# One PSUM tile with five banks, against separate PSUM tiles and another fixed order

## The chip, the cores and the metric

The kernel runs on one core of a Trainium2 chip. The time is device microseconds of one execution. Before the change, three executions took 315.47, 315.55 and 319.2 us, a median of 315.55 us. One of them was recorded by the profiler; all durations below come from that one.

## What is computed

A retention layer with a recurrent state, then a layer norm without offset, a two-layer perceptron with ReLU, and a residual. Inputs are float32.

```
q, k, v: (4, 8, 768, 64)             # batch, heads, sequence, head dim
gamma = 1 - 2 ** (-5 - arange(8))    # one per head
for t in range(768):
    state = gamma * state + k[t] (outer) v[t]
    y[t] = q[t] @ state / 8
x = y as (4, 768, 512)
xn = (x - mean) / sqrt(var + 1e-6) * g_ln
out = x + relu(xn @ w_ch1) @ w_ch2   # 512 -> 2048 -> 512
```

## The kernel before

**Tiles.** A batch has 6 chunks of 128 positions, so there are 24 tiles. Tiles 0 to 3 are the first chunks of the four batches, 4 to 8 are chunks 1 to 5 of batch 0, 9 to 13 those of batch 1, and so on.

**The steps of one tile t.** Loads of q, k, v go out on POOL's queue (float32 to bfloat16 in the DMA, L422); later ones are paced by a one-element copy on POOL that waits for an earlier load (L435). Tiles 0 to 7 have q and k transposed on TensorE (L488, L495) and evacuated by VectorE with a scaling (eq, L500) and by ACT (ek, L250). From tile 8 on SP transposes them by DMA (tr, L510) and VectorE scales (eq, L517). Then:

- *pa*: the scores, eight matmuls with 64 rows, two heads at a time, into two banks (L528).
- *am*: VectorE multiplies the scores by a decay mask into `asb` (L553).
- *ps*: from tile 8 on, the state's part of y, eight matmuls with 64 rows and 64 columns that stand ahead of pa and write the two banks of y (L539). Tiles 4 to 7 have it as four full-row matmuls in py (L575).
- *py*: eight matmuls that add the scores times v (L564; L579 up to tile 7).
- *bn*: VectorE's statistics of y (L595, L596). *xn*: VectorE's normalisation without the 1/sqrt (L607). *xc*: ACT copies y into `x_all`, for the residual (L614). From tile 8 on, y lies in two banks, so that bn, xn and xc have two instructions each.
- *vg*, *pd*, *pb*: POOL scales v (L628), TensorE adds the chunk's k times v into the state's bank (L640), VectorE scales that into one of two `state` tiles for the next chunk (L654).
- *tx*, *ex*: up to tile 7 xn is transposed on TensorE (L667) and copied by ACT (L250); later SP transposes it by DMA into `xnt` (L681).

**The perceptron.** Tiles go in groups: eight of one tile, four of two, two of four. M1 multiplies w1 by a group's xnt, in units of four 512-column matmuls' worth, into one of two `mm` buffers (L714), and ACT, or VectorE for some early ones, writes the ReLU into `h1` (L727, L729). M2 multiplies a tile's h1 by w2, sixteen matmuls in four quarters of four (L752), into one bank. Then *add* (L762) applies the 1/sqrt of the group (L689, L695), adds `x_all` and writes `osb`, and SP stores it (L769). The last tile's M2 is cut in 384 and 128 columns.

**PSUM.** `pd` has one bank, `mm` two. The other five are slices of a single tile, `banks`, with the names b0, b1, b2, p0, p1:

```
BANKS = ("b0", "b1", "b2", "p0", "p1")
TWO = [("b0", "b1")]
banks = ctx.enter_context(tc.tile_pool(name="banks", bufs=1, space=ps)).tile(
    [P, len(BANKS), 4 * P], FP32, name="banks")
```

pa takes p0 and p1. py takes b2 up to tile 7 and b1 and b2 after. The transposes take b0 or b1. M2 takes b0 or b1 for tiles 0 to 3, b0 for tiles 4 to 15 and any of the five from tile 16 on; which one is a digit of the order.

**The order.** Every step is a task given to `Plan.add` with its engine, a duration, what it comes after and which buffers it uses. A list of numbers, `ORDER`, says in which order the tasks of all engines, loads included, are written down. `Plan.order` walks through it with a small model of times and buffers, and `Plan.fill` uses these times to put matmuls on zeros (`warm`, L780) into TensorE's idle time in the first 14 us. Each engine runs its tasks in that order. The waits between engines are put in by the tile framework, by the tiles that instructions read and write; the plan's own list of what a task comes after makes none.

Of the kernel before, what the change touches and what calls it, by code (L numbers as in the profile page):

```python
# [22 lines left out]
    "load_pad": 600, "w_pad": 550, "lead": 32, "lead2": 32, "sq_at": 28000, "late_load": 1250, "two": 4, "m2b": ("b0",), "m2all": 16, "inter": 4, "every": 4, "tail": (0, 384, 512), "step": 8, "pace": 8, "ahead": 3,  # L23
# [6 lines left out]
3 2 15 18 19 23 24 0 5 6 4 8 7 16 20 1 17 22 14 21 10 27 26 25 146 100147 29 30 9 148  # L30
149 11 150 162 153 44 100163 151 28 13 32 164 45 33 154 100176 165 155 152 156 179 177
166 100158 157 167 168 159 31 178 214 169 170 100190 180 191 193 12 100172 171 524 181
192 46 174 173 182 183 194 532 204 34 184 35 36 47 38 100186 215 207 187 10525 10533 39
37 534 217 185 40 42 49 41 234 50 542 48 205 195 51 206 196 535 526 543 540 52 197 527
251 53 198 10541 54 43 208 55 216 528 209 200 544 100224 199 529 10545 201 188 227 536
537 225 226 210 550 175 211 552 228 212 229 551 553 546 220 213 221 218 100241 10547 219
548 242 556 10549 230 275 560 243 244 231 232 235 557 558 236 56 245 561 559 554 59 57
233 555 237 246 58 268 60 530 100258 247 238 562 531 248 570 252 259 261 563 249 260 566
571 564 262 239 567 254 565 250 160 256 255 568 538 100716 263 10569 253 10539 717 718
722 264 61 719 723 62 161 189 265 63 64 298 65 66 266 287 720 269 724 725 578 100271 726  # L40
572 727 721 307 276 267 270 728 272 202 573 579 278 299 277 279 67 71 729 730 731 280
574 72 576 300 222 575 240 732 281 734 282 284 288 223 577 203 283 735 736 273 285 290
68 289 69 70 301 291 737 584 582 738 292 302 740 741 77 742 293 743 294 295 296 297 585
78 73 74 303 308 75 318 319 310 309 322 744 580 286 746 333 311 304 76 83 747 312 320 84
79 581 748 305 583 749 313 314 588 316 315 745 733 339 317 334 602 323 325 589 750 324
592 752 80 350 603 753 257 335 326 81 306 327 328 329 331 600 754 340 82 755 593 739 321
354 85 601 351 586 330 89 332 337 587 342 756 86 341 90 87 758 594 88 91 368 595 92 336
95 596 379 93 338 352 96 343 344 274 355 345 94 346 382 97 98 99 101 102 380 348 397 759
100 760 590 761 597 347 103 349 357 591 107 356 598 381 762 358 610 764 359 599 360 361
765 766 383 604 767 362 363 369 364 371 751 386 403 370 611 763 384 768 614 605 372 608  # L50
770 373 771 374 375 398 609 615 606 366 377 757 353 365 376 618 378 772 387 389 388 390
108 104 607 619 773 105 774 404 106 113 414 418 775 612 616 109 110 114 429 111 112 115
391 116 456 119 392 120 117 776 613 617 393 395 118 394 620 777 396 622 621 623 399 406
405 778 626 407 415 408 419 409 410 627 433 624 625 412 779 416 628 634 401 411 769 145
385 417 445 413 400 421 420 430 121 122 123 125 126 780 127 782 783 629 635 422 431 367
423 784 630 424 785 425 427 426 428 631 124 632 131 132 129 459 402 434 457 786 436 435
788 437 432 465 789 646 633 438 128 476 130 647 790 650 133 458 446 439 440 791 441 442
443 651 638 448 792 447 449 639 640 460 794 461 641 781 444 450 466 451 452 454 480 644
645 795 453 477 796 636 455 468 467 797 637 478 469 642 648 462 643 798 137 134 138 491
143 135 139 136 492 470 800 495 787 471 481 793 140 472 474 649 473 652 475 653 801 802  # L60
662 483 663 482 666 803 667 658 484 506 659 141 485 142 144 656 804 806 657 486 496 487
488 489 493 654 660 807 490 655 661 498 497 808 809 510 499 479 799 511 463 670 671 810
500 664 507 824 665 501 502 503 504 668 508 672 505 669 513 673 512 825 674 678 464 514
515 300818 675 826 679 676 400812 677 682 680 813 819 814 494 516 683 681 517 519 509
518 521 684 686 520 685 687 815 690 805 811 691 696 820 697 702 522 694 703 695 100830
704 705 827 831 698 699 688 689 821 706 707 200854 692 816 523 822 693 708 300848 832
828 710 833 709 700 701 836 711 400842 849 843 712 714 850 837 817 823 829 715 713 834
838 839 851 855 844 845 852 856 840 835 853 857 846 860 841 861 847 862 858 863 864 859
865
# [3 lines left out]
class Plan:  # L73
# [6 lines left out]
    def __init__(self, seen, begin, first_load):  # L80
        self.seen, self.begin, self.first_load = seen, begin, first_load
        self.tasks, self.bufs, self.chosen = [], {}, {}
# [4 lines left out]
    def add(self, eng, ns, rank, emit, after=(), takes=None, uses=(), load=0, hw=0, lat=0, at=0,  # L87
            follows=(), slack=0, slots=None):
        after = [d for x in after for d in (x if isinstance(x, list) else [x])]
        t = {"on": eng if isinstance(eng, dict) else {eng: ns}, "rank": rank, "emit": emit,  # L90
             "after": after, "takes": takes, "uses": list(uses) + ([takes] if takes else []),
             "slots": (slots or [(takes[0],)]) if takes else [],
             "load": load, "hw": hw, "lat": lat, "at": at, "follows": list(follows),
             "slack": slack}
        self.tasks.append(t)
        return t

    def order(self, seq):
# [7 lines left out]
        for number in seq:  # L106
# [7 lines left out]
            for options in t["slots"]:  # L114
# [20 lines left out]
            for name in got:  # L135
# [3 lines left out]
                self.chosen[t["takes"]] = name  # L139
# [21 lines left out]
def kernel(  # L161
# [33 lines left out]
    T0, TX, T_TWO = CFG["T0"], CFG["TX"], CFG["two"]  # L195
# [16 lines left out]
    BANKS = ("b0", "b1", "b2", "p0", "p1")  # L212
    TWO = [("b0", "b1")]

    def make_pool(name, n, space=None):
# [7 lines left out]
        for name, n, space in (  # L223
# [3 lines left out]
            ("pd", 1, ps), ("mm", 2, ps),  # L227
        )
    }
    for name in BANKS:  # L230
        plan.pool(name, 1)
    plan.pool("pb", 2)
    held = {}
    banks = ctx.enter_context(tc.tile_pool(name="banks", bufs=1, space=ps)).tile(
        [P, len(BANKS), 4 * P], FP32, name="banks")

    def bank(key, bf16=False):
        x = banks[:, BANKS.index(plan.chosen[key])]
        held[key] = x.bitcast(BF16)[:, 0:4 * P].rearrange("p (i t) -> p i t", t=P) if bf16 else x
        return held[key]  # L240
# [4 lines left out]

    def heads(x):
        return x.rearrange("p (i a d) -> p i a d", a=2, d=D)
# [28 lines left out]
    bns = const.tile([P, NT, 2, 6], FP32, name="bns")  # L276
    mv = const.tile([P, NT, 2], FP32, name="mv")
    touch = const.tile([P, KO, 1], FP32, name="touch")
# [172 lines left out]
    a(SP, 390, -140, lambda eng: nc.sync.dma_start(out=touch, in_=w1_v[:, :, 0:1]), hw=300)  # L451

    unit, u, behind = {}, 0, []
    for g in range(NG):
        for ho in range(HO):
            unit["1", g, ho] = u
            u += GROUPS[g] / 4
            every = CFG["every"] if GROUPS[g] == 1 else 8 if 12 <= G0[g] < 16 and GROUPS[g] == 2 else 4
            if g >= CFG["inter"] and ho % every == every - 1 and behind:
                unit["2", behind.pop(0)] = u  # L460
                u += 4
# [14 lines left out]
    for t in range(NT):  # L476
# [7 lines left out]
        if t < T0:  # L484
            def e_tk(eng, t=t):
                p = bank(("tp", ("k", t)), True)
                for i in range(NPAIR):
                    nc.tensor.transpose(p[:, i, :], tile_of("k", t)[:, 2 * i:2 * i + 2, :], idn)  # L488
            tk = a(PE, 230, r - 0.1, e_tk, [loaded["k", t], ident] + ([tq] if tq else []),
                   ("tp", ("k", t)), [where["k", t]], slots=TWO)  # L490

            def e_tq(eng, t=t):
                p = bank(("tp", ("q", t)), True)
                for i in range(NPAIR):
                    nc.tensor.transpose(p[:, i, :], tile_of("q", t)[:, 2 * i:2 * i + 2, :], idn)  # L495
            tq = a(PE, 230, r, e_tq, [loaded["q", t], ident, tk], ("tp", ("q", t)),
                   [where["q", t]], slots=TWO)
# [25 lines left out]
        def e_pa(eng, t=t):  # L523
            pa = held["pa", t] = banks[:, 3:5].rearrange("p a (i t) -> p a i t", t=P)
            for i in range(NPAIR):
# [6 lines left out]
        pat = a(PE, 410, r + 1.2, e_pa, [eq, ek], ("pa", t), [("trq", t), kt], slack=slack,  # L532
                slots=[("p0",), ("p1",)])

        def e_ps(eng, t=t):
            for i in range(NPAIR):
                for par in range(2):
                    o = slice(D * par, D * (par + 1))
                    nc.tensor.matmul(  # L539
                        banks[:, 1 + par, i * D:(i + 1) * D], lhsT=held["trq", t][o, i, :],  # L540
                        rhs=held["pb", t][o, i, o], start=(i == 0), stop=False)
        pst = None
        if t >= T0:
            pst = a(PE, 120, r + 1.1, e_ps, [eq] + ([pbt[t]] if c > 1 else []), ("py", t),
                    [("trq", t), ("pb", t)], slots=[("b1",), ("b2",)])
            pat["after"].append(pst)
# [13 lines left out]
        def e_py(eng, t=t, c=c):  # L560
            if t >= T0:
                held["py", t] = banks[:, 1:3, 0:NPAIR * D].rearrange("p a (i d) -> p i a d", d=D)
                for h in range(H):
                    nc.tensor.matmul(  # L564
                        banks[:, 1 + h % 2, h // 2 * D:(h // 2 + 1) * D],
# [34 lines left out]
        for a2 in (range(2) if late else [None]):  # L600
            def e_xn(eng, t=t, a2=a2):
                if not a2:
                    take("xn", t, [P, DM], BF16)
# [212 lines left out]
```

## Time and profile before

| | |
|---|---|
| time of the profiled execution | 315.47 us |
| its span, first to last instruction | 313.7 us |
| granted TensorE clock, mean | 0.951 |
| asb, L553, x24 | 1223 ns each |
| osb (add), L762, 512 columns, x23 | 749 ns each |
| xn, L607: 512 columns x8; 256 columns x32 | 751; 481 ns each |
| bns, L595: 512 columns x8; 256 columns x32 | 698; 422 ns each |
| mv, L596: one part x8; two parts x16 | 182; 209 ns each |
| x_all, L614: 512 columns x8; 256 columns x32 | 588; 374 ns each |
| M2, L752, 512 columns, x368 | 389 ns each, mean |
| load of a part of w to landing, x8, median | 8.4 us |
| tr; xnt by DMA to landing, median | 3.6; 2.4 us |

A row of a group gives the line in the kernel, the engine, the operation, what it writes and reads, how often, its busy time and the mean of one. PE is TensorE's matmuls, PEld its weight loads, DVE VectorE, ACT ScalarE, POOL GpSimd, SP the sync engine's queue. Matmuls are pipelined and their ends are modelled: a single 512-column matmul reads some 380 ns while the next one starts 216 ns later. Idle time of an engine is given with the last thing that it waited for, as "X <- Y", or in brackets in the timeline.

### The profile page before, as it was taken

Reading aid. Unit: us, or ns where it says so; the run is one execution under the profiler, and the core shown is the slowest. Engines: PE = TensorE matmul, PEld = TensorE weight load, DVE = VectorE, ACT = ScalarE, POOL = GpSimd, SP = SyncE. Lnnn points to the kernel's source line nnn. Section 1 sums busy time; section 2 is a strip of 40 time slices with the busy share of each in tenths; the row PEclk is TensorE's granted clock in tenths of the full one; section 3 lists DMA queues with packets and bytes.
Section 4 is the critical chain, followed back from the end, with each engine's and each line's share of the span. In section 5 each row is a group of like instructions: output and inputs, shape, how many; then the busy total and the mean of one; then the engine's idle time right before and its main releaser. Section 6 shows DMA issues by size and latency. Waiting matters only on the chain. (4 is left out here: it accounts for less than half of the span.)

```text
span 313.7 us, 4959 instructions
## 1 busy us (share of the span) xinstructions
PE 230.5 (73%) x2029; PEld 141.6 (45%) x2029; DVE 124.7 (40%) x265; ACT 81.9 (26%) x170; POOL 97.5 (31%) x151
## 2 busy tenths in 40 slices
PE   3964676788867576768678687676977887699973
PEld 1433575677444244525446464444633433244431
DVE  3423445562454325544426454647326342002013
ACT  3122233246003202203103333213322232243200
POOL 9985561257014056406423533423000000000000
PEclk9997579999999997978999999999999999799999
DMA  9999998099209159969929996884910000201013
GB/s 135 169 187 171 199 163 101 3 69 70 17 20 163 20 35 159 123 75 117 100 84 87 87 133 84 67 103 61 176 50 11 8 17 0 87 0 67 33 37 134
DMA packets 108890, 26.82 MB, mean 85 GB/s; under 512 B 101569, under 2 KB 105921, under 8 KB 108866
## 3 DMA queue, kind: packets, MB, share of 16 engines
q0 software_dynamic: 77024, 13.37, 54.5%
q1 hardware_dynamic: 30642, 12.79, 18.7%
q10 hardware_dynamic: 1200, 0.33, 0.5%
q8 instruction: 16, 0.26, 0.4%
q14 instruction: 8, 0.07, 0.1%
HBM read 27.27 MB, written 6.29 MB: 107 GB/s over the span
## 5 line engine op out<-in xcount | busy, mean ns | idle before, releaser
L752 PE MATMUL banks<-w,h 128*128 128x512 bf16 (+2 forms) x400 | 97.1, 380 | 32.0 <-DVE xn L607 9.2
L714 PE MATMUL mm<-xnt,w 128*128 128x128 bf16 (+2 forms) x896 | 101.8, 268 | 7.3 <-DMA xnt<-xn 4.7
L714 PEld LDWEIGHTS <-w 128*128 128x128 bf16 x896 | 70.4, 103 | 30.8 <-issue 10.3
L727 ACT ACTIVATE h<-mm 128x512 bf16<-128x512 f32 x88 | 51.3, 600 | 84.9 <-PE mm L714 84.9
L752 PEld LDWEIGHTS <-h 128*128 128x128 bf16 x400 | 38.0, 99 | 75.3 <-issue 41.9
L553 DVE TENSOR_TENSOR asb<-banks,mask 128x1024 bf16<-128x1024 f32 x24 | 29.4, 1223 | 53.1 <-PE banks L752 31.6
L628 POOL TENSOR_TENSOR vg<-vsb,vsc 128x512 bf16<-128x512 bf16 x16 | 16.6, 1038 | 95.2 <-PE pd L640 86.0
L762 DVE SCALAR_TENSOR_TENSOR osb<-banks,rstd,x_all 128x512 f32<-128x512 f32 (+2 forms) x25 | 18.2, 728 | 60.5 <-ACT h L727 25.8
L614 ACT CAST x_all<-banks 128x256 bf16<-128x256 f32 (+1 forms) x40 | 15.8, 417 | 96.5 <-PE banks L752 28.6
L595 DVE BATCH_NORM_STATS2 bns<-banks 128x6 f32<-128x256 f32 (+1 forms) x40 | 17.8, 477 | 38.9 <-PE banks L752 26.9
L607 DVE SCALAR_TENSOR_TENSOR xn<-banks,mv,gb 128x256 bf16<-128x256 f32 (+1 forms) x40 | 20.5, 535 | 17.2 <-ACT x_all L614 7.3
L422 POOL DMA_DIRECT2D vsb<-in_v_dram x20 | 18.1, 908 | 1.5 <-issue 1.4
L654 DVE TENSOR_TENSOR state<-pd,gch 64x256 bf16<-64x256 f32 x40 | 16.7, 417 | 1.9 <-PE pd L640 1.5
L422 POOL DMA_DIRECT2D qk<-in_q_dram x16 | 14.5, 908 | 1.0 <-issue 0.8
L422 POOL DMA_DIRECT2D qk<-in_k_dram x16 | 14.3, 893 | 0.9 <-issue 0.8
L250 ACT COPY trk<-banks 128x512 bf16<-128x512 bf16 x8 | 4.7, 587 | 24.7 <-PE banks L488 7.9
L539 PE MATMUL banks<-state,trq 64*128 64x64 bf16 x128 | 4.9, 194 | 7.9 <-ACT x_all L614 5.6
L564 PE MATMUL banks<-vsb,asb 128*128 128x64 bf16 x128 | 6.4, 193 | 5.0 <-DVE asb L553 3.5
L780 PE MATMUL pd<-zeros 128*128 128x512 bf16 (+1 forms) x27 | 8.8, 481 | 1.2 <-DVE zeros L285 1.2
L564 PEld LDWEIGHTS <-asb 128*128 128x128 bf16 x128 | 5.5, 98 | 9.1 <-DVE asb L553 6.6
L539 PEld LDWEIGHTS <-trq 64*128 64x128 bf16 x128 | 3.7, 95 | 12.6 <-issue 7.0
L528 PE MATMUL banks<-trq,tr 64*128 64x128 bf16 x128 | 6.6, 222 | 2.7 <-DVE osb L762 2.7
(68 smaller groups left out, 140.7 us busy)
## 6 DMA issues: line engine op xcount, KB each, us to landing
out_dram<-osb SPq DMA_DIRECT2D x23, 256.0 KB, 2.3
w<-in_moe_w_ch_dram POOLq DMA_DIRECT2D x8, 512.0 KB, 8.4
vsb<-in_v_dram POOLq DMA_DIRECT2D x20, 128.0 KB, 4.5
qk<-in_k_dram POOLq DMA_DIRECT2D x16, 128.0 KB, 3.8
qk<-in_q_dram POOLq DMA_DIRECT2D x16, 128.0 KB, 3.7
qsb<-in_q_dram POOLq DMA_DIRECT2D x7, 128.0 KB, 7.2
v<-in_v_dram POOLq DMA_DIRECT2D x4, 128.0 KB, 5.7
ksb<-in_k_dram POOLq DMA_DIRECT2D x4, 128.0 KB, 8.6
```

Of the source, the lines that this page charges most:

```text
L422: nc.gpsimd.dma_start(out=tile_of(kind, j), in_=src)
L553: nc.vector.tensor_tensor(out=take("asb", t, [P, NPAIR, 2, P], BF16).rearrange("p i a t -> p a i t"), in0=held["pa", t], in1=mask.rearrang ...
L564: nc.tensor.matmul(banks[:, 1 + h % 2, h // 2 * D:(h // 2 + 1) * D], lhsT=held["asb", t][:, h // 2, h % 2, :], rhs=tile_of("v", t)[:, h, : ...
L595: nc.vector.bn_stats(out=bns[:, t, i, :], in_=x)
L607: nc.vector.scalar_tensor_tensor(out=dst, in0=src, scalar=mv[:, t, 0:1], in1=g, op0=ALU.subtract, op1=ALU.mult)
L614: nc.scalar.copy(out=dst, in_=src)
L628: e.tensor_tensor(out=take("vg", j, [P, H, D], BF16), in0=tile_of("v", j), in1=vsc[:, cc, :].unsqueeze(2).to_broadcast([P, H, D]), op=ALU. ...
L654: nc.vector.tensor_tensor(out=held["pb", n][o, :, o], in0=held["pd", b][o, :, o], in1=gch[o, cc, :].unsqueeze(2).to_broadcast([D, NPAIR, D ...
L714: nc.tensor.matmul(p[:, j, :], lhsT=w1[:, ko, (ho + j) * P:(ho + j + 1) * P], rhs=held["xnt", hb][:, h0:h0 + n, ko, :], start=(ko == 0), s ...
L727: nc.scalar.activation(out=dst, in_=src, func=AF.Relu)
L752: nc.tensor.matmul(held[key][:, 0:w], lhsT=held["h1", hb][:, ho, i * P:(i + 1) * P], rhs=w2[:, ho, cols], start=(ho == 0), stop=(ho == HO ...
L762: nc.vector.scalar_tensor_tensor(out=take("osb", key, [P, w], FP32), in0=held[key][:, 0:w], scalar=rstd[:, t:t + 1], in1=x_all[:, t, cols] ...
```

## The change

- The tile `banks` goes. Three pools come in its place: `tp` with two banks (transposes and all of M2), `pa` with one buffer of two banks, `py` with one bank. With `pd` and `mm` that makes eight banks, as before. `Plan` loses the choice of a bank (`slots`, `chosen`), and the settings `two`, `m2b`, `m2all`, `inter` and `every` go.
- y lies in one bank for every tile. The task ps goes; from tile 4 on py has the four full-row state matmuls itself. bn, xn and xc are one task each with 512 columns.
- The ranks that M2 tasks get (`unit`) are worked out in another way; with a fixed `ORDER` they move nothing.
- `ORDER` is another list, and with it the order on every engine, of the loads and of the gates. POOL's first load is k of tile 1; w2's last part stands behind vg of tile 1. The number of warm matmuls follows from the plan.
- The load named `touch` takes 16 columns of w1 where it took 1, and stands elsewhere on SP's queue.

```diff
 ORDER = [int(x) for x in """
-3 2 15 18 19 23 24 0 5 6 4 8 7 16 20 1 17 22 14 21 10 27 26 25 146 100147 29 30 9 148
+15 18 14 23 3 8 19 2 27 24 13 26 22 25 44 16 17 45 0 4 7 6 5 28 146 20 21 9 147 10 149 1
...
-            ("pd", 1, ps), ("mm", 2, ps),
+            ("tp", 2, ps), ("pa", 1, ps), ("py", 1, ps), ("pd", 1, ps), ("mm", 2, ps),
...
-    banks = ctx.enter_context(tc.tile_pool(name="banks", bufs=1, space=ps)).tile(
-        [P, len(BANKS), 4 * P], FP32, name="banks")
...
-    a(SP, 390, -140, lambda eng: nc.sync.dma_start(out=touch, in_=w1_v[:, :, 0:1]), hw=300)
+    a(SP, 390, -140, lambda eng: nc.sync.dma_start(out=touch, in_=w1_v[:, :, 0:16]), hw=400)
...
-                p = bank(("tp", ("k", t)), True)
+                p = take("tp", ("k", t), [P, NPAIR, P], BF16)
...
-            pa = held["pa", t] = banks[:, 3:5].rearrange("p a (i t) -> p a i t", t=P)
+            pa = take("pa", t, [P, 2, NPAIR, P], FP32)
...
-        def e_ps(eng, t=t):
-            for i in range(NPAIR):
-                for par in range(2):
-                    o = slice(D * par, D * (par + 1))
-                    nc.tensor.matmul(
-                        banks[:, 1 + par, i * D:(i + 1) * D], lhsT=held["trq", t][o, i, :],
-                        rhs=held["pb", t][o, i, o], start=(i == 0), stop=False)
...
-            py = bank(("py", t)).rearrange("p (h d) -> p h d", d=D)
+            py = take("py", t, [P, H, D], FP32)
             n = H + (NPAIR if c > 0 else 0)
             mi = 0
             if c > 0:
                 for i in range(NPAIR):
                     nc.tensor.matmul(py[:, 2 * i:2 * i + 2, :], lhsT=held["trq", t][:, i, :],
                                      rhs=held["pb", t][:, i, :], start=(mi == 0), stop=False)
                     mi += 1
...
+        def e_xn(eng, t=t):
+            nc.vector.scalar_tensor_tensor(
+                out=take("xn", t, [P, DM], BF16), in0=held["py", t].rearrange("p h d -> p (h d)"),
+                scalar=mv[:, t, 0:1], in1=gb, op0=ALU.subtract, op1=ALU.mult)
+
         def e_bn(eng, t=t):
-            parts = [banks[:, 1 + a, 0:NPAIR * D] for a in range(2)] if t >= T0 else [
-                held["py", t].rearrange("p i a d -> p (i a d)")]
-            for i, x in enumerate(parts):
-                nc.vector.bn_stats(out=bns[:, t, i, :], in_=x)
-            nc.vector.bn_aggr(out=mv[:, t, :], in_=bns[:, t, 0:len(parts), :])
+            nc.vector.bn_stats(out=bns[:, t, :], in_=held["py", t].rearrange("p h d -> p (h d)"))
+            nc.vector.bn_aggr(out=mv[:, t, :], in_=bns[:, t, :])
...
+        def e_xc(eng, t=t):
+            nc.scalar.copy(out=x_all[:, t, :].rearrange("p (h d) -> p h d", d=D),
+                           in_=held["py", t])
...
             def e_m2(eng, hb=hb, i=h0 + i4, key=key, part=part, cols=cols, w=w):
                 if part == 0:
-                    bank(key)
+                    take(*key, [P, w], FP32)
```

## The prediction

> **What bounds the kernel now.** I read the page first, its busy table and its 40 slices (7.84 us each):
>
> ```profile
> PE 230.5 (73%) x2029; PEld 141.6 (45%) x2029; DVE 124.7 (40%) x265; ACT 81.9 (26%) x170; POOL 97.5 (31%) x151
> ...
> PEclk9997579999999997978999999999999999799999
> DMA  9999998099209159969929996884910000201013
> ```
>
> then the busy times of three stretches, cut where the first M2 matmul starts (79.23 us) and where the last group's M1 starts (269.32 us); after each engine's busy time come clock, DMA share, GB/s:
>
> ```profile
> core 0: us, PE busy (x) PEld busy (x) DVE busy (x) ACT busy (x) POOL busy (x), PEclk, DMA share, GB/s
> 0.00:79.23 79.23, 53.67 (x653) 42.65 (x654) 32.84 (x75) 27.36 (x55) 48.48 (x71) 0.89 1.33 126
> 79.23:269.32 190.09, 139.53 (x1204) 82.11 (x1202) 85.70 (x180) 44.99 (x98) 48.98 (x80) 0.97 0.63 75
> 269.32:313.70 44.38, 37.26 (x176) 16.88 (x176) 6.19 (x10) 9.52 (x17) 0.00 (x0) 0.96 0.16 57
> ```
>
> No engine is full, and after 47 us the DMA engines are not either. TensorE is nearest, and 50.5 of its 83 idle us lie in the middle stretch. So I asked for whom it waits there (engine, line, who was waited for: total us, times, longest):
>
> ```profile
> PE banks L752 <- DVE xn L607: 9.2, 7, 1.8
> PE banks L752 <- DVE asb L553: 8.5, 8, 1.4
> PE banks L752 <- ACT x_all L614: 5.6, 6, 2.0
> PE banks L539 <- ACT x_all L614: 5.6, 7, 1.4
> PE mm L714 <- DMA xnt<-xn: 4.7, 1, 4.7
> PE banks L564 <- DVE asb L553: 3.5, 4, 1.3
> PE banks L752 <- DVE osb L762: 2.8, 2, 2.2
> PE banks L528 <- DVE osb L762: 2.7, 3, 0.9
> PE pd L640 <- DVE state L654: 2.4, 1, 2.4
> PE banks L752 <- DVE bns L595: 1.7, 2, 0.9
> ```
>
> L752 is M2. It multiplies h1 by w2 into a bank of its own; nothing in it needs the scores (asb), the normalised rows (xn), the copy x_all or the statistics (bns) of another tile, which lie in other banks. All five banks are slices of one tile, `banks`, and the program waits per tile. The built instruction list confirms it: of 34 M2 waits on VectorE's counter, 24 stand at a later quarter of a tile, where the bank is already held. The clearest place is after the last y (L564, ended 256.88):
>
> ```profile
> 256.48 0.40 PE L564 MATMUL banks<-vsb,asb 128*128 128x64 bf16 x8
> ...
> 264.68 0.76 DVE L595 BATCH_NORM_STATS2 bns<-banks 128x6 f32<-128x256 f32 x2 [8.43 <-PE banks L752]
> ...
> 269.32 2.29 PE L714 MATMUL mm<-xnt,w 128*128 128x512 bf16 x5 [4.67 <-DMA xnt<-xn]
> ```
>
> VectorE could have read y at 256.9; it waited until unrelated M2 matmuls ended, 7.8 us later. M1, which needs what follows, then idled 4.67 us.
>
> **The change, part by part.**
>
> *Pools for the one tile.* Scores, y, and the transposes with M2 get tiles of their own. In the changed program's list M2 has 22 waits on VectorE, each at a tile's first quarter, on the add that frees its bank. Waits of asb, bns, xn on M2 go from 25 to 0, those of ACT's copies from 20 to 0. Gone in the middle: 9.2+8.5+5.6+1.7 = 25.0 at M2; 2.2 of the 2.8 on osb (one quarter mid-tile); 2.7 (L528 on osb, another bank) and a 1.5 (L564 on osb); the 4.7 on xnt, which followed from the late statistics. Sum 36.1 us. In the tail L752 waits for osb five times, 4.1 us, again at later quarters or another bank, and M1 ran its first eight matmuls in 3.4 us at half clock after the idle 4.67, against 1.73 for later eights: 1.7 us. What is next where a stall goes: TensorE's own next task, since the order lists M1 or M2 quarters there.
>
> *State part of y.* Before, eight 64-row matmuls (L539), 0.12 us from their start to the scores' start. After, four full-row ones ahead of y, as L575 in tiles 4 to 7: y with them takes 0.46 us to the next task, without 0.23. So +0.11 us on TensorE for each of 16 tiles, +1.8 us.
>
> *One bank for y.* VectorE drops from 2x0.422+0.209 to 0.698+0.182 for statistics and from 2x0.481 to 0.751 for xn; ACT from 2x0.374 to 0.588. That is 6.1 and 2.6 us less in all, beside TensorE: counted nothing. It would cost something if the y bank came free too late. It is held 0.88+0.75+0.59 = 2.2 us after y, 3.5 with an asb (1.22) in between; from tile 8 on the changed order has at least five M1 units or M2 quarters (4.3 us) between two y, seven in the mean, so 0.8 us are over in the tightest tile. The Trainium skill (PSUM — Partial Sum Buffer, PSUM bank collisions raise a hardware error) says that two engines must not touch one bank at once, reads included, which speaks against one bank, since ACT cannot copy while VectorE reads. No run here shows a collision. By that rule each tile's chain grows by ACT's 0.59 us, and with none of it hidden the sum would be 9 us higher.
>
> *Orders.* TensorE's work splits alike: 24 M1 units (before: up to the first M2 at 79.2 us; after: up to the scores of tile 8), then 56 M1 units and 72 M2 quarters up to the last group's M1, then 16 and 24 (a unit is 4 matmuls of 512 columns; the chain has eight in 1.73 us, so 0.865; with 256 columns 0.87, with 128 0.89). Warm-up matmuls go from 27 to 32, in the idle start. POOL's gates and loads move: the last load of w2 now stands behind vg of tile 1, which waits for pd of tile 5; that comes mid-start, and M2 needs w2 only after the scores of tile 8: nothing, or the load's 8.4 us if that cover were gone. SP's touch DMA grows from 1 to 16 columns and moves ahead of the output of tile 1 and the transpose of tile 12; it took 4.9 us to land, so at worst these are 5 us late, two tiles ahead of use: nothing. A transfer that ends late elsewhere would stop TensorE for at most what the transposes take, 3.6 us (tr) or 2.4 (xnt) each.
>
> *Sum, by stretch.* The profiled execution took 315.47 us, 1.8 more than its span; the median is 315.55, the same.
> Start: 79.2, and 0.7 for y and pd of tile 7, which come first now: 79.9. Waits on other banks there come to 10.4 us (L488 on xn 2.8 and asb 0.5, L495 on asb 0.5, L667 on asb 2.4 and xn 0.8, L575 and L579 on trq 2.3, L528 on bns and xn 1.1), but the DMA row stands at 9 for six slices and the clock is at 0.5 from 30 to 40 us, so loads bound part of it; I take back 4.4: 75.5 (72 to 80).
> Middle: 128 units x 0.87 = 111.4; 16 scores and y x (0.33+0.46) = 12.6; 15 pd x 0.22 = 3.3; one transpose 0.2: 127.5. To it, waits that are real. Before, 50.5-36.1 = 14.4 us were left, part of them at L539, which goes. Two stretches of the new order done by hand with the rows above (tiles 13 to 15 and 16 to 18) show none: asb ends 4 us ahead of its y. I take 10 (bounds 0 and 20: 14.4 and 0.17 us for each of some 30 waits, a 512-column matmul's 0.38 us in the trace against 0.216 apart).
> Clock: from 118 to 146 us it went down to 0.5 (120 to 122) and 0.63 to 0.76 (132 to 142); busy time times the missing share makes 4.0 us, and I take 3, since fewer waits may leave it up longer. The skill (TensorE: Matmul & The Clock Gate, Part 1) puts half clock behind an idle window of some 3.4 us. Here it fell with no idle over 2.4 us before it, and at 132 to 142 with none over 1.4, so they differ and the rows decide. By the rule this term would be 0 and the sum 3 us lower.
> Tail: 40 units x 0.866 = 34.6, and 3.0 from the last M2 matmul to the end of the span (313.7 - 310.7), as before.
> 75.5+127.5+10+3+34.6+3.0+1.8 = **255 us**.
>
> **The rivals.**
> *Only the direct waits go.* If loads and latencies bound the rest: 315.5-36.1-4.1-1.7+1.8 = 275 us, down to 270 with the start's half. For it: VectorE and ACT were late in many places, and I can't show that the rest shrinks. Against: the hand-done tiles.
> *Two tp banks become the bound.* M2 took any of five banks in the end; now each tile waits for the add two tiles back. If each of 24 starts cost 1.4 us (the longest wait on asb): 255+34 = 289, less if hidden. Against: VectorE is 45% busy there.
> *Nothing changes.* The waits might come from the chip's in-order counters rather than the shared tile: 315 us. Against: the list of waits.
> *Slower.* One pa and one y tile make a serial chain score, asb, statistics, xn, copy: 1.22+0.88+0.75+0.59 and four handovers of 0.1 = 3.8 us. TensorE would idle that long per tile if the order laid nothing between. It decides from (321.9-242)/24 = 3.3 us per tile on (242 is the sum without the 10 and the 3); whole, it gives 242+24x3.8 = 333 us. Against: the new order lays three to nine units between scores and y.
>
> **How the numbers follow.** The forecast (245 to 267) gets 0.64, the direct waits alone (268 to 276) 0.21, the two banks 0.06, no change 0.04, slower 0.05. The low end: start 72, 3 us of waits and no clock loss give 242, rarely reached, so 245; the high end is the second case's 276. That range holds some 0.82. Two per cent, 309.2 to 321.9, is about what a measurement can tell from no change. Faster is 0.64+0.21+0.06 = 0.91, same 0.04, slower 0.05.
>
> **What would show it.** Waits of M2 only on osb; bns starting 0.1 us after y; the last group's M1 without a wait on xnt; the tail near 37.6 us; the middle near 141. It is wrong if M2 still waits for asb or xn, if the start stays at 80, or if eq or pa waits for tr in most tiles.

## The result, and the profile after

The changed kernel takes 224.14 us (median of six runs, 222.9 to 229.31) against 315.77 us for the kernel before beside it: a ratio of 0.709 [0.705, 0.712]. Some executions of every kernel take a few per cent longer than its others; medians and ranges here are over all executions, ratios over the shorter ones alone. That is faster, as forecast, but 31 us below the forecast and 21 us below the low end of its range. The profiled execution took 224.2 us, with a span of 222.4 us.

The page of the kernel after, its busy table and three of its rows of 40 slices (5.56 us each):

```profile
PE 208.9 (94%) x1970; PEld 135.0 (61%) x1970; DVE 118.6 (53%) x230; ACT 82.2 (37%) x157; POOL 97.3 (44%) x151
...
PE   3798899994999999998999999999999999999994
...
PEclk9999999998899999999999999999999999999999
DMA  9999999999399999999999999699940112002032
```

TensorE is now the bound: 94% busy, and its row reads 9 nearly everywhere after the ninth slice. Its granted clock has two slices under 9, where it had seven before. Its busy time itself fell, from 230.5 to 208.9 us, though its work is nearly the same.

The same three stretches of the kernel after, cut where the scores of tile 8 start (24 M1 units done) and where the last group's M1 starts:

```profile
core 0: us, PE busy (x) PEld busy (x) DVE busy (x) ACT busy (x) POOL busy (x), PEclk, DMA share, GB/s
0.00:53.45 53.45, 43.51 (x674) 36.47 (x675) 35.76 (x82) 28.84 (x59) 38.76 (x53) 1.00 1.58 156
53.45:184.66 131.21, 130.63 (x1121) 81.99 (x1121) 77.21 (x140) 43.61 (x81) 58.58 (x98) 0.99 1.13 123
184.66:222.40 37.74, 34.73 (x177) 16.56 (x175) 5.67 (x10) 9.74 (x17) 0.00 (x0) 1.00 0.17 63
```

Against 79.23, 190.09 and 44.38 us, the start lost 25.8 us, the middle 58.9 and the tail 6.6. In the middle TensorE is idle for 131.21 - 130.63 = 0.6 us in all. The forecast had 75.5, 140.5 and 37.6: the tail is right, the middle is 9.3 us too long, and the start is 22.0 us too long.

TensorE's waits in the kernel after, all of the list (who waited, for whom: total us, times, longest):

```profile
PE tp L468 <- ACT k L231: 3.3, 1, 3.3
PE pa L508 <- DVE trq L497: 3.1, 1, 3.1
PE pd L722 <- DVE zeros L266: 1.2, 1, 1.2
PE mm L657 <- DMA w<-in_moe_w_ch_dram: 0.9, 1, 0.9
PE mm L657 <- DMA xnt<-xn: 0.6, 1, 0.6
PE tp L610 <- DVE xn L546: 0.6, 1, 0.6
PE pd L582 <- issue: 0.4, 1, 0.4
PE mm L657 <- ACT h L670: 0.4, 1, 0.4
```

M2 (now L695) is not in it. The place shown before, after the last y, now reads so in the timeline (start, us, engine and line, what it writes and reads; in brackets the idle time ahead of it):

```profile
176.65 0.40 PE L536 MATMUL py<-vsb,asb 128*128 128x64 bf16 x8
...
177.09 0.70 DVE L551 BATCH_NORM_STATS2 bns<-py 128x6 f32<-128x512 f32 x1 [1.05 <-PE py L536]
...
178.82 1.19 SPq L624 DMA_TRANSPOSE xnt<-xn  x1
...
184.66 1.67 PE L657 MATMUL mm<-xnt,w 128*128 128x512 bf16 x7
```

VectorE reads y 0.04 us after its last matmul, where it was 7.8 us; the transposition goes out early, and M1 at 184.66 us has no idle time ahead of it.

### The profile page after: what moved, and what is told of

Its sections match the earlier page's. It is cut to its first block, busy times and chain, and to the rows that moved or that the text cites. A ratio compares the mean times of both kernels' runs of the same rounds, so it can differ in the third digit from the quotient of the medians.

```text
span 222.4 us, 4762 instructions
## 1 busy us (share of the span) xinstructions
PE 208.9 (94%) x1970; PEld 135.0 (61%) x1970; DVE 118.6 (53%) x230; ACT 82.2 (37%) x157; POOL 97.3 (44%) x151
## 4 chain that ended last, share of the span: by engine, by line
PE 70%; DMA 18%; POOL 8%; issue 2%; DVE 1%; POOLq 0%
PE tp L695 36%; PE mm L657 27%; DMA tr<-qk 7%; DMA w<-in_moe_w_ch_dram 5%; DMA xnt<-xn 3%; DMA qk<-in_q_dram 2%; PE pa L508 2%; PE py L536 2%; POOL qsb L403 2%; PE pd L582 2%; PE py L532 2%; POOL k L403 1%; POOL v L403 1%; POOL w L411 1%; POOL vg L570 1%
## 5 line engine op out<-in xcount | busy, mean ns | idle before, releaser
L657 PE MATMUL mm<-xnt,w 128*128 128x128 bf16 (+2 forms) x896 | 97.6, 260 | 1.8 <-DMA w<-in_moe_w_ch_dram 0.9
L695 PE MATMUL tp<-w,h 128*128 128x512 bf16 (+2 forms) x400 | 92.1, 371 | 0.0
L695 PEld LDWEIGHTS <-h 128*128 128x128 bf16 x400 | 37.0, 98 | 36.3
L704 DVE SCALAR_TENSOR_TENSOR osb<-tp,rstd,x_all 128x512 f32<-128x512 f32 (+2 forms) x25 | 18.1, 726 | 32.3 <-PE tp L695 32.1
L519 DVE TENSOR_TENSOR asb<-pa,mask 128x1024 bf16<-128x1024 f32 x24 | 29.3, 1220 | 9.3 <-PE pa L508 9.0
L551 DVE BATCH_NORM_STATS2 bns<-py 128x6 f32<-128x512 f32 x24 | 16.7, 695 | 19.1 <-PE py L536 19.1
L557 ACT CAST x_all<-py 128x512 bf16<-128x512 f32 x24 | 14.0, 583 | 22.6 <-DVE xn L546 20.1
L546 DVE SCALAR_TENSOR_TENSOR xn<-py,mv,gb 128x512 bf16<-128x512 f32 x24 | 18.0, 749 | 0.7
L416 POOL COPY scrap<-qk 1x1 bf16<-1x1 bf16 x30 | 5.4, 179 | 17.7 <-DMA qk<-in_q_dram 8.9
L497 DVE TENSOR_TENSOR trq<-tr,qsc 128x512 bf16<-128x512 bf16 x16 | 7.9, 496 | 4.8 <-DMA tr<-qk 4.7
L508 PE MATMUL pa<-trq,tr 64*128 64x128 bf16 x128 | 6.4, 219 | 3.1 <-DVE trq L497 3.1
## 6 DMA issues: line engine op xcount, KB each, us to landing
w<-in_moe_w_ch_dram POOLq DMA_DIRECT2D x8, 512.0 KB, 10.4
```

Of the source, the lines that this page charges most:

```text
L508: nc.tensor.matmul(pa[:, par, i, :], lhsT=held["trk", t][o, i, :] if t < T0 else held["tr", t][o, NPAIR + i, :], rhs=held["trq", t][o, i, ...
L519: nc.vector.tensor_tensor(out=take("asb", t, [P, NPAIR, 2, P], BF16).rearrange("p i a t -> p a i t"), in0=held["pa", t], in1=mask.rearrang ...
L546: nc.vector.scalar_tensor_tensor(out=take("xn", t, [P, DM], BF16), in0=held["py", t].rearrange("p h d -> p (h d)"), scalar=mv[:, t, 0:1], ...
L551: nc.vector.bn_stats(out=bns[:, t, :], in_=held["py", t].rearrange("p h d -> p (h d)"))
L557: nc.scalar.copy(out=x_all[:, t, :].rearrange("p (h d) -> p h d", d=D), in_=held["py", t])
L657: nc.tensor.matmul(p[:, j, :], lhsT=w1[:, ko, (ho + j) * P:(ho + j + 1) * P], rhs=held["xnt", hb][:, h0:h0 + n, ko, :], start=(ko == 0), s ...
```

## The experiments

Stages are given as start, middle and tail: up to 24 M1 units done, up to the last group's M1, up to the end of the span. "One execution" is a single time.

**1. The kernel before with a tile for each bank.** Order, structure, bank choice and instructions stay as they were; b0, b1 and b2 become tiles of their own, and p0 with p1 a fourth.

```diff
-    banks = ctx.enter_context(tc.tile_pool(name="banks", bufs=1, space=ps)).tile(
-        [P, len(BANKS), 4 * P], FP32, name="banks")
+    single = {x: ctx.enter_context(tc.tile_pool(name=x, bufs=1, space=ps)).tile(
+        [P, 4 * P], FP32, name=x) for x in BANKS[:3]}
+    both = ctx.enter_context(tc.tile_pool(name="both", bufs=1, space=ps)).tile(
+        [P, 2, 4 * P], FP32, name="both")
+
+    def bank_of(i):
+        return single[BANKS[i]] if i < 3 else both[:, i - 3]
...
-        x = banks[:, BANKS.index(plan.chosen[key])]
+        x = bank_of(BANKS.index(plan.chosen[key]))
```

> The kernel before with its own order, its 64-row state part and y over two banks, but b0, b1 and b2 each a tile of its own and p0 with p1 a fourth. Theory A (the waits through the one tile are the whole loss, in the start too): the start up to the first M2 falls from 79 us to about 53, the middle from 190 to about 130, the tail from 44 to 38, together 220 to 230 us; TensorE waits in M2 for asb, xn, bns and x_all vanish. Theory B (the new order, of loads and tasks, gives the 22 us of the start that the prediction missed): the start stays at 70 us or more and the time is 245 us or more. Theory C (y in one bank matters): 255 us or more, with waits of TensorE on the y banks.

Measured: 222.64 us, ratio 0.701 [0.694, 0.709]. Its stretches:

```profile
0.00:48.98 48.98, 41.79 (x654) 35.30 (x655) 34.18 (x78) 27.34 (x55) 35.28 (x50) 1.00 1.68 166
48.98:183.00 134.02, 130.12 (x1204) 79.41 (x1202) 82.51 (x178) 46.36 (x98) 63.01 (x102) 0.99 1.20 123
183.00:222.30 39.30, 34.89 (x177) 16.52 (x175) 5.92 (x10) 9.52 (x17) 0.00 (x0) 1.00 0.15 54
```

This edit alone gives the whole gain. The start fell by 30.2 us with every load in its old place, so the loads had not bounded it. (The profiled execution took 224.05 us; the others 227.67, 221.23 and 219.49.)

**2. The kernel after, with its five banks as slices of one tile again.** The new order and the one y bank stay.

```diff
-            ("tp", 2, ps), ("pa", 1, ps), ("py", 1, ps), ("pd", 1, ps), ("mm", 2, ps),
+            ("pd", 1, ps), ("mm", 2, ps),
...
+    banks = ctx.enter_context(tc.tile_pool(name="banks", bufs=1, space=ps)).tile(
+        [P, 5, 4 * P], FP32, name="banks")
...
+            if pool == "pa":
+                x = banks[:, 3:5].rearrange("p a (i t) -> p a i t", t=P)
+            elif pool == "py":
+                x = banks[:, 2].rearrange("p (h d) -> p h d", d=D)
+            else:
+                x = banks[:, len(turn) % 2]
```

> The changed kernel with its own order, y in one bank and the full-row state part, but tp, pa and py as slices of one tile of five banks. Theory A: M2 again waits for asb, xn, bns and x_all, some 40 us of such waits or more, and the time is 300 us or above. Theory B (the order avoids them): 250 us or less.

Measured: 321.45 us (one execution), stages 75.7, 200.9 and 43.1, mean clock 0.89. TensorE's waits in it (M2 is L710 here):

```profile
PE banks L710 <- DVE osb L719: 16.3, 12, 2.5
PE banks L710 <- DVE asb L534: 12.9, 7, 3.5
PE banks L710 <- DVE xn L561: 6.7, 6, 1.9
PE banks L547 <- ACT x_all L572: 5.6, 3, 4.3
```

M2 waits for scores and normalised rows again; with 2.6 us for x_all and 2.1 for the statistics, which the list has further down, that is 24.3 us, less than the some 40 us expected, while the time is as expected. The new order does not avoid the cost of the shared tile; the separate tiles do.

**3 and 4. Part of the sharing, and one y bank.** In the third kernel only b0, M2's main bank, leaves the shared tile of the kernel before.

```diff
+    lone = ctx.enter_context(tc.tile_pool(name="lone", bufs=1, space=ps)).tile(
+        [P, 4 * P], FP32, name="lone")
...
-        [P, len(BANKS), 4 * P], FP32, name="banks")
+        [P, len(BANKS) - 1, 4 * P], FP32, name="banks")
...
-        x = banks[:, BANKS.index(plan.chosen[key])]
+        i = BANKS.index(plan.chosen[key])
+        x = banks[:, i - 1] if i else lone
```

> The kernel before with only b0 taken out of the shared tile; b1, b2, p0, p1 stay one tile. Theory A: M2 of tiles 4 to 15 is free of other banks, so the middle falls by about 25 of its 60 lost us, the last group waits for its M1 still, since M2 of tiles 16 on uses all banks, and transposes in b1 keep half of the start's waits: 265 to 290 us. Theory B: 300 us or more.

Measured: 242.21 us (one execution), a miss: lower than any theory had it. Stages 63.5, 135.0 and 41.9. Freeing this one bank gave back 72 of the 91 us. The wait at the last group's M1, where the statistics are late, is still there:

```profile
PE mm L717 <- DMA xnt<-xn: 4.7, 1, 4.7
```

The fourth is the first one with y in one bank and its state part as four full-row matmuls, as in the kernel after.

```diff
-            pst = a(PE, 120, r + 1.1, e_ps, [eq] + ([pbt[t]] if c > 1 else []), ("py", t),
+            pst = a(PE, 120, r + 1.1, lambda eng: None, [eq] + ([pbt[t]] if c > 1 else []), ("py", t),
...
-            py = bank(("py", t)).rearrange("p (h d) -> p h d", d=D)
+            py = bank_of(2).rearrange("p (h d) -> p h d", d=D)
...
-            for i, x in enumerate(parts):
-                nc.vector.bn_stats(out=bns[:, t, i, :], in_=x)
+            nc.vector.bn_stats(out=bns[:, t, 0, :], in_=parts[0])
```

> As the kernel before with own tiles, and besides y of every tile in bank b2 alone, its state part as four full-row matmuls in y, and statistics, xn and copy in one instruction each; the order stays the one of before. Theory A: the row prices, 0.11 us more on TensorE for 16 tiles and 6 us less on VectorE beside it, so within 3 us of the kernel before with own tiles. Theory C: at least 8 us away from it.

Measured: 221.26 us, ratio 0.702 [0.695, 0.709], the same as the first within the intervals. Beside TensorE, one y bank costs nothing that can be told.

**5 and 6. Which sharing costs what.** The fifth is the first one with b0, p0 and p1 as one tile, so that M2 shares with the scores; the sixth has b1 and b2, the two banks of y, as one.

```diff
+    trio = ctx.enter_context(tc.tile_pool(name="trio", bufs=1, space=ps)).tile(
+        [P, 3, 4 * P], FP32, name="trio")
+
+    def bank_of(i):
+        return single[BANKS[i]] if 1 <= i < 3 else trio[:, max(0, i - 2)]
```

```diff
+    pair = ctx.enter_context(tc.tile_pool(name="pair", bufs=1, space=ps)).tile(
+        [P, 2, 4 * P], FP32, name="pair")
...
+    def bank_of(i):
+        return lone if i == 0 else pair[:, i - 1] if i < 3 else both[:, i - 3]
```

> The kernel before with own tiles (b0, b1, b2, and p0 with p1), except that b0, the bank of the transposes and of M2 for tiles 4 to 15, shares one tile with the score banks p0 and p1. Theory A (each shared pair brings its own waits): only the waits between M2 or transposes and asb come back; in the kernel before these were 8.5 us of TensorE's and 31.6 us of VectorE's waiting, so 235 to 255 us, the start 52 to 60 us. Rival D (waits hide behind each other, and one shared pair is enough to lose most of it): 280 us or more. Rival E (TensorE finds other work): below 228 us.

> The kernel before with own tiles, except that b1 and b2 share one tile. From tile 8 on both hold the same y, up to tile 7 b1 holds transposes and b2 holds y. Theory A: the middle stays within 4 us of 134, its two xn and x_all halves wait for each other again (VectorE's wait for x_all, 7.3 us before, comes back in part), and the start grows from 49 to 53 to 60 us; 225 to 234 us. Rival D: 250 us or more.

Measured: 235.56 us (stages 53.1, 141.4, 39.3) and 227.27 us (57.7, 128.5, 39.3), one execution each. The fifth is as expected. The sixth is so in its total and its start; its middle lies 5.5 us below the 134 us of the first kernel, whose profile holds a wait for an output buffer there (see 7, 9 and 10). In the fifth, the waits of the scores' evacuation and of M2 show both directions of the coupling:

```profile
PE trio L758 <- DVE asb L558: 6.6, 5, 1.3
...
DVE asb L558 <- PE trio L758: 23.2, 10, 4.5
```

TensorE waits 6.6 us in M2 for scores to be read, and VectorE 23.2 us where it may not read scores until M2 matmuls end. The first kernel's four executions lie between 219.49 and 227.67 us. Against them the two banks of y in one tile (sixth, 227.27) can't be told from separate ones by the total, though the start is 8.7 us longer (57.7 against 49.0). M2's bank with the scores (fifth) costs 7.9 to 16.1 us, the four banks without b0 (third) 14.5 to 22.7, and all five some 91 (313.89 beside them). So most of the loss came only with all five in one tile. I put that down to hardly two engines being able to work on any of the banks at once; that is argued, not shown.

**7, 9 and 10. More buffers for the output.** In the tail of the fourth kernel the timeline of VectorE has

```profile
215.66 1.01 DVE L756 SCALAR_TENSOR_TENSOR osb<-b,rstd,x_all 128x384 f32<-128x384 f32 x2 [0.89 <-DMA out_dram<-osb]
```

so the last add waits 0.89 us for a store to free one of three `osb` buffers. The first kernel's profile has a longer such wait in its middle, which reaches M2:

```profile
158.86 0.75 DVE L768 SCALAR_TENSOR_TENSOR osb<-b,rstd,x_all 128x512 f32<-128x512 f32 x1 [5.36 <-DMA out_dram<-osb]
...
159.66 1.02 PE L758 MATMUL b<-w,h 128*128 128x512 bf16 x4 [3.64 <-DVE osb L768]
```

The seventh kernel is the fourth with six, the ninth the first with six, and the tenth the kernel after with six:

```diff
-            ("xn", 4, None), ("xnt", 4, None), ("h1", 2, None), ("osb", 3, None),
+            ("xn", 4, None), ("xnt", 4, None), ("h1", 2, None), ("osb", 6, None),
```

> As own tiles with y in one bank in the order of before, and six osb buffers in place of three. There the last tile's add waited 0.89 us for a store to free its buffer, and 4.2 us passed from the last M2 matmul to the end of the span, 3.0 in the changed kernel. If that wait is on the last path: 0.5 to 1 us less, 219 to 221 us; if the stores themselves end the span: no change, 220 to 222 us.

> The kernel before with own tiles, its 64-row state part and y over two banks, and six osb buffers. Against the one with y in one bank and six osb buffers (219.4 us): by the row prices the 64-row state part saves 0.11 us of TensorE for 16 tiles, 1.8 us, which is on the path now that TensorE is 95% busy: 217 to 218.5 us. If one bank or two does not matter at all: 219 to 220. If the shared tile of p0 and p1 or the second halves of xn and x_all cost something: 220 or more.

> The changed kernel with six osb buffers in place of three. Its tail shows no wait for an osb buffer, and 3.0 us from the last M2 matmul to the end: no change, 223 to 225 us. If a wait for osb is hidden elsewhere: 1 to 2 us less.

Measured: 219.42 us (219.23 to 219.54), ratio 0.700 [0.695, 0.704], for the seventh; 218.3 us (217.95 to 218.72), 0.696 [0.692, 0.699], for the ninth; 0.711 [0.704, 0.719] for the tenth, no change against the kernel after. The intervals of the seventh and the ninth overlap those with three buffers (fourth and first), so a gain is not shown by the times alone; the waits are gone from the profiles. M2 waits for osb for 0.2 us in all in the seventh and in the ninth, and in the seventh the same add starts at 213.42 us with no wait:

```profile
213.42 0.92 DVE L756 SCALAR_TENSOR_TENSOR osb<-b,rstd,x_all 128x384 f32<-128x384 f32 x2
```

The ninth is the best of all and beats both kernels: the order and structure of before, a tile for each bank, six output buffers. Its interval lies below the tenth's, so the change's order and structure together are worth less than nothing beside separate tiles: 223.3 - 218.3 = 5.0 us lost, by the three shortest executions of the tenth (223.24, 223.3, 223.64; the others took 227.06 and 230.55). The profile of the kernel after shows where. Two lines of its timeline at the end of the start, and the two stretches behind:

```profile
52.97 0.42 DVE L497 TENSOR_TENSOR trq<-tr,qsc 128x512 bf16<-128x512 bf16 x1 [4.74 <-DMA tr<-qk]
...
53.45 0.40 PE L508 MATMUL pa<-trq,tr 64*128 64x128 bf16 x8 [3.13 <-DVE trq L497]
```

```profile
54.00:56.00 2.00, 2.00 (x24) 2.00 (x22) 1.94 (x8) 0.58 (x1) 0.00 (x0) 0.52 1.84 129
56.00:58.00 2.00, 2.00 (x21) 1.85 (x20) 1.13 (x1) 0.15 (x1) 0.04 (x1) 0.63 0.34 30
```

The transposition by DMA for tile 8 went out at 38.44 us and was 14.5 us in landing (the median of its sixteen is 4.6). TensorE waited 3.1 us for it, and then ran at a clock of 0.52 and 0.63 for 4 us: 2 x 0.48 + 2 x 0.37 = 1.7 us more. The ninth kernel has no wait of TensorE for a DMA of any kind. That these 4.8 us are the whole of the 5.0 was not tested by itself: other executions with the new order wait elsewhere too, once for an `xnt`, 5.6 us in the tenth kernel (its profile is of the 227.06 us), 4.4 in the eighth, 2.4 in the eleventh. With the waits for trq, w and xnt together, TensorE waits 4.6 us for what a DMA brings in the kernel after, 4.7 in the eleventh, 6.6 in the eighth and 6.9 in the tenth.

**8 and 11. Small parts of the change.** The eighth is the kernel after without its 32 warm matmuls, which write nothing that is used; the eleventh takes `touch` back to one column.

```diff
-        for t in plan.fill(plan.order(ORDER), PE, 1100, FILL_END, FILL, warm):
+        for t in plan.order(ORDER):
```

```diff
-    a(SP, 390, -140, lambda eng: nc.sync.dma_start(out=touch, in_=w1_v[:, :, 0:16]), hw=400)
+    a(SP, 390, -140, lambda eng: nc.sync.dma_start(out=touch, in_=w1_v[:, :, 0:1]), hw=300)
```

> The changed kernel without the 32 matmuls on zeros. It tests the step of the prediction that took the half clock of the start for a bound of its own. If the clock follows how continuously TensorE works: it falls below 1 in the first 20 us here too and the first M1 units take 1.7 us in place of 0.9, 2 to 5 us more than the changed kernel's 224. If the real work keeps it up: within 1 us, clock 1 from 10 us on.

> The changed kernel with the touch load of 1 column, as before, in place of 16. The prediction counted it nothing, at worst 5 us late for transfers two tiles ahead: no change, 223 to 225 us. If the load's size delayed the transposes behind it: 1 us less or more.

Measured: 227.06 us (one execution) and 222.9 us, ratio 0.709 [0.703, 0.715]. The eleventh shows no change that can be told. In the eighth the clock row reads 1.00 in each of the first four 10 us, but the matmuls don't bear it out: an early M1 unit (the first line, from the eighth) takes nearly twice as long as in the kernel after (the second), as the first of the two expectations had it.

```profile
16.23 1.90 PE L657 MATMUL mm<-xnt,w 128*128 128x128 bf16 x16
...
16.49 1.06 PE L657 MATMUL mm<-xnt,w 128*128 128x128 bf16 x16
```

Four transposes take 0.61 us at 18.60 us in the eighth and 0.39 from 22.34 us on; in the kernel after they take 0.39 from 9.93 us on. So the warm matmuls brought the full pace some 11 us earlier. They made no shorter start: its 25th M1 unit starts at 53.0 us (54.0 in the kernel after), in both kernels behind a wait for the transposition of tile 8 (2.2 and 3.1 us). The 3 us more are in one wait of M1 later, which other runs of this order have too:

```profile
PE mm L657 <- DMA xnt<-xn: 4.4, 1, 4.4
```

One execution can't say whether leaving them out brings that wait.

## Why the prediction was right in kind and wrong in size

*The cause was right.* The step that M2 waits for work in other banks because the five share a tile was read from the list of waits; experiment 1 shows it by undoing it alone (0.701), experiment 2 by putting it back (321 us). "Nothing changes", "two tp banks" (M2 has no wait on osb), and "slower" fell: the chain of score, asb, statistics, xn and copy stays hidden in experiment 4, too. "Only the direct waits go" fell on the other side.

*The start is the step that failed.* It said: "Waits on other banks there come to 10.4 us [...], but the DMA row stands at 9 for six slices and the clock is at 0.5 from 30 to 40 us, so loads bound part of it; I take back 4.4: 75.5". It came to 53.5, and to 49.0 in experiment 1. Two things were wrong in it. First, the 10.4 us were only those of TensorE's waits on other banks that VectorE ended. The list of the same 79.23 us of the kernel before has four more that ACT's copies ended, 6.6 us together:

```profile
PE banks L495 <- ACT trk L250: 3.8, 2, 3.1
...
PE banks L579 <- ACT xnt L250: 1.2, 1, 1.2
PE banks L488 <- ACT xnt L250: 0.9, 1, 0.9
...
PE banks L667 <- ACT trk L250: 0.7, 1, 0.7
```

Experiment 1, with the same banks in the same order, has none of the four. That makes 17.0 us in place of 10.4, and TensorE's idle time of the start fell by 18.4 us there (25.6 to 7.2). ACT itself was held in the same way; its list for this stretch has

```profile
ACT trk L250 <- PE banks L667: 5.9, 1, 5.9
ACT trk L250 <- PE banks L495: 5.5, 2, 4.0
...
ACT x_all L614 <- PE banks L667: 4.7, 3, 2.4
ACT x_all L614 <- PE banks L488: 4.6, 1, 4.6
ACT trk L250 <- DVE trq L500: 4.1, 2, 3.5
```

That is 24.8 us of ACT's waiting, and ACT copies the transposes that M1 and the scores need; how much of it reached TensorE beyond the waits above is not shown. trk, a copy of transposed k, has no use for L495 (q), L667 (xn) or trq. In the kernel after, ACT's list for its start has of these two steps only waits for the bank that they read themselves, x_all's for VectorE's read of it:

```profile
ACT x_all L557 <- DVE xn L546: 5.0, 3, 2.3
...
ACT trk L231 <- PE tp L468: 1.9, 2, 1.6
```

Second, I took busy DMA engines and a low clock for bounds of their own. After, the DMA row reads 9 for ten slices, 55.6 us, longer than before, and TensorE's work of the start is done within them. TensorE's waits for a DMA in them are 0.9 us for a part of w and, at their end, 3.1 us by way of trq; 3.3 us more pass at the start for the first k. The clock was a consequence: experiment 1 changed the tiles alone and the start's clock went from 0.89 to 1.00. Of the 25.8 us that went, 15.6 were idle time (25.6 to 9.9) and 10.2 busy time (53.67 to 43.51). The missing clock of before from 20 to 50 us (0.84, 0.50, 0.81 on 5.49, 6.84 and 7.35 us busy) makes 5.7 of the 10.2. The rest fits the clock as well, where the clock row leaves it out: it reads 1.00 from the first instruction on, while early matmuls read long. Four transposes still take 0.63 us in the kernel before at

```profile
22.08 0.63 PE L667 MATMUL banks<-idn,xn 128*128 128x128 bf16 x4
```

and in experiment 1 they take 0.39 us already at

```profile
11.51 0.39 PE L500 MATMUL b<-idn,qsb 128*128 128x128 bf16 x4
```

The kernel before was busy for 8.88 us from 10 to 22.5 us. At about half pace that is an estimated 4.4 us too many, and 10.2 - 5.7 leaves 4.5.

*The middle was 9.3 us too long*, for the same reason: I took 10 us of real waits where 0.6 were left, and left 3 us for a clock that cost 1.7. The term of pure work, 127.5 us, was 1.4 us short: 130.6 busy, less the 1.7, is 128.9. The two stretches that I had worked out by hand showed no wait, and I put in 10 from what remained of the stalls of before all the same; those too were consequences of the shared tile.

*Small terms.* The tail, 37.6 us, came to 37.74. The state part was priced at 1.8 us for full rows; the seventh kernel is 1.1 us above the ninth, with runs that don't overlap, though in two sets beside befores of 315.81 and 315.54. One y bank was counted nothing, and it was. That two engines' reads of one bank would come one after the other, with 9 us if nothing hid it, was the rule set against it: in the built list the copy x_all does wait for xn in all 24 tiles, though both only read y, and none of it reaches TensorE. `touch` was counted nothing, and no cost of it can be told (experiment 11). The order was counted at nothing for its transfers, with 3.6 us (tr) or 2.4 (xnt) at most for each that comes late. That bound was too low, since it took the usual time to landing: one tr took 14.5 us, and a wait on xnt reached 5.6.

## What to carry to other kernels

In this framework a PSUM tile is the unit of waiting, for reads and for every engine: give each bank that is used by itself a tile of its own, and look in the list of waits for readers that wait for work whose data they never touch. When such a false wait goes, count it whichever engine ended it, and look at every engine of the chain and not only at the one that bounds the kernel, and don't take a low clock, busy transfers or leftover stalls of the old profile as floors for the new one until something shows that they are. Measure an order found offline beside the old order with the same fix in both: here the fix was all of the gain, and the new order and structure together lost 5 us of it. Where a clock row reads 1.00 from the start, compare early matmuls with later ones of the same shape before believing it.

## What the runs showed of the hardware

The record shows the clock fall in two settings. The first is a single gap in otherwise full work. After 3.1 us (kernel after), after 3.6 us (experiment 1: 0.73, 0.50 and 0.92 in the two-us windows from 160 us on) and around the wait of 4.4 us (eighth: 0.80, 0.50, 0.84 from 102 us on) the missing clock adds up to 1.7 us each time, as of some 3.4 us at half. Around 5.6 us (tenth) it read 0.50 from 100 to 106 us; after the waits of 2.1 and 2.4 us of the eleventh it stayed at 1.00. The second is work with many waits: in the start of the kernel before it read 0.50 from 28 to 42 us, around a gap of 2.8 us, and the third and the sixth kernel have it at 0.50 around gaps of 2.5 us. Ahead of its first change the row reads 1.00 in every kernel, and there the durations of the matmuls count: four transposes read 0.61 to 0.63 us up to 8 us in the kernel after, 19 us in the eighth and 22 us in the kernel before, and 0.39 at full pace. The Trainium skill (TensorE: Matmul & The Clock Gate, Part 1) puts a half clock behind an idle window of some 3.4 us, which is near to these single gaps. In the middle of the kernel before it fell with no gap over 2.4 us; the same part also tells of clocks that swing where TensorE idles briefly between groups of matmuls while it goes through PSUM banks, and the kernel before agrees with that: with the short waits taken out, nothing else changed, the mean of the clock row went from 0.951 to 0.992.
